# Another order of TensorE's work items in a segment-recurrent attention kernel on Trainium2

## The chip, the cores and the metric

One Trainium2 chip, of which the kernel uses one core. The metric is the time of one execution in device microseconds (us), and less is better. A core has five engines, each with an instruction queue of its own that is worked off in program order: TensorE (PE; its weight loads are listed as PEld), VectorE (DVE), ScalarE (ACT), GpSimd (POOL) and SyncE (SP), which issues most of the DMA transfers. They meet at semaphores: an instruction waits until those that produce its data, or free its buffer, have signalled. Matmul operands lie in the on-chip memory ("arena" in the trace), results in eight PSUM banks ("ps"), and 16 DMA engines carry data between the chip's HBM and the arena.

## What is computed

A memory-augmented attention layer and a gated feed-forward layer, mixed by a gate, over x of shape (1, 2048, 640) in bf16. The attention goes through 64 segments of 32 rows. Each puts 8 memory rows in front of its own (L = 40 rows), and its first 8 output rows are the memory of the next one, so segment s + 1 can't start its products before segment s has ended.

```python
for s in range(n_seg):                       # 64 segments, 32 heads of 192
    h = jnp.concatenate([mem, x[:, 32 * s:32 * s + 32, :]], axis=1)
    q, k, v = (jnp.einsum('btd,dhe->bhte', h, W) for W in (Wq, Wk, Wv))
    scores = jnp.einsum('bhqe,bhke->bhqk', q, k) * Dh ** -0.5
    scores = jnp.where(mask[None, None], scores, -1e9)
    o = jnp.einsum('bhqk,bhke->bhqe', softmax(scores), v)
    o = jnp.einsum('bhte,hed->btd', o, Wo)
    mem = o[:, :8, :]
    outs.append(o[:, 8:, :])
g = sigmoid((x * gate_w).sum(-1, keepdims=True))
out = g * concat(outs) + (1 - g) * ((gelu(x @ w_gate) * (x @ w_up)) @ w_down)
```

## The kernel before

The feed-forward layer is computed first, up to about 170 us. Then come the 64 segments, in groups of four. Segment s has the **type** s mod 4, and a planned order of TensorE items: the list `PROG` for types 0, 1 and 2, the list `PROG3` for type 3 (lines 524 to 545). `segment(s)` walks through the list, and each item emits its instructions on all engines that it concerns. Two items that are neighbours in the list follow each other on TensorE, and the copies and softmax steps that they emit stand in the same order on ScalarE, VectorE and GpSimd. A list is thus the schedule of every engine.

A tile has 32 columns and a segment 40 rows. The 8 memory rows and 24 of the segment's own go through the products of the segment itself; the other 8 own rows of each of a group's four segments, 32 in all, depend on x alone and make one block, the **left rows**, whose products are worked out ahead of the group.

The 32 heads are four **octets** of eight; octet numbers in the items count positions (0 to 3) in the segment, and the real octets come in reverse order in odd segments. The items:

- `g` n,k: slice k (0 to 4) of the contraction over 640, for product group n of `GROUPS`: group 0 is Q and K of octet 0; 1 is V 0, Q 1, K 1; 2 is V 1, Q 2, K 2; 3 is V 2, Q 3; 4 is K 3; 5 is V 3. A **product** is four matmuls of 128x384, one on each 32-column tile of the array (lines 1132, or 226 where the stationary operand is kept from the product before). Behind k = 4, ScalarE copies the results out of PSUM (line 1153 for Q and K, 1156 for V).
- `tq` i, `tk` i: VectorE transposes the Q or K rows of octet i into one buffer `Qs` or `Ks` (line 1170). As there is only one of each, the `tk` of the next octet waits for the scores of this one.
- `sc` i: mask (line 1181) and scores (1189, 234, 1196) of octet i on 64-column tiles, then maximum and subtraction on VectorE. `ex` i: the exponential on ScalarE (1220), then sum, reciprocal and two multiplications on VectorE (1222 to 1227).
- `pt` i: transposes of the probabilities (1243, 1248), copied out by ScalarE (1261; for the last octet half of it by VectorE). `pv` i: probabilities times V on 64-column tiles (1276, 1278), copied out by ScalarE (1308; for the last octet in halves, 1298 and 1302).
- `wo` i,h: half of octet i's part of the output product, in 32-column tiles for types 0 to 2 (lines 1326, and 1352 for the last octet), in 64-column tiles for type 3 (1370).
- `lf` t,u,k: done only in type t. A **left pair**, that is a Q and a K product (lines 924 and 226) for the left rows of a later group. `le` t,u,m: copy and transpose of such rows (1398). `vb` k, type 3 only: the V product of the next group's left rows for octet 0 (965).

In type 0 the product groups with V of octets 1 to 3 carry one product more per slice, that of the left rows, so that a slice of group 2 has four products and one of group 3 has three.

A segment ends with the last `wo`, the addition of partial sums and two transposes (1570) on VectorE, on which the next segment's first `g` waits. The `lf` and `le` items at the end of a list lie in that wait; `le` items behind the last `wo` are emitted after the segment's end steps.

Not all weights fit on chip. Of each pair of first-octet and fourth-octet pieces, 13 of Q, K, V (384 KB each) and three of Wo (480 KB) share a slot: as soon as an item has used up a piece that has a partner, `swap_loads` puts the partner's load into SyncE's queue (`load_piece`, line 629). So the fourth octet's K and V and the last Wo pieces of a segment are loaded within that segment, in the order in which the first octet's pieces come free, and its items wait for their landing.

```python
def swap_loads(seg, item):
    ...
    for key in done_keys:
        other = swap_in.get(key)
        if other is None or (other in partner) == (seg % 2 == 0):
            continue
        load_piece(other, "swap s%d" % seg)
```

Of the kernel before, what the change touches and what calls it, by code (L numbers as in the profile page):

```python
# [238 lines left out]
def _build(nc, A_x, A_mem0, A_Wq, A_Wk, A_Wv, A_Wo, seg_len, w_gate, w_up, w_down,  # L239
# [278 lines left out]
    def piece_view(key, o):  # L518
        if key[0] == 3:
# [1 line left out]
        return bview(o, GQ)  # L521

    GROUPS = [[(0, 0), (1, 0)], [(2, 0), (0, 1), (1, 1)], [(2, 1), (0, 2), (1, 2)], [(2, 2), (0, 3)], [(1, 3)], [(2, 3)]]
    PROG = [("g", 0, 0), ("g", 0, 1), ("g", 0, 2), ("g", 0, 3), ("g", 0, 4), ("tq", 0), ("g", 1, 0), ("g", 1, 1),
# [12 lines left out]
    PROG3 = [("g", 0, 0), ("g", 0, 1), ("g", 0, 2), ("g", 0, 3), ("g", 0, 4), ("g", 1, 0), ("tq", 0), ("tk", 0),  # L537
# [8 lines left out]
    PROGS = (PROG, PROG, PROG, PROG3)  # L546
    assert NOCT == 4
    WOP = 4
# [1065 lines left out]
def bass_gated_mix__memory_aug_recurrent_mem_tr__glu_gated_geglu__prompt_kernel(  # L1614
    nc,
    A_x,
    A_mem0,
    A_Wq,
    A_Wk,
    A_Wv,  # L1620
    A_Wo,
    A_seg_len,
    B_x,
    B_w_gate,
    B_w_up,
    B_w_down,
    gate_w,
    out,
):
    _build(nc, A_x, A_mem0, A_Wq, A_Wk, A_Wv, A_Wo, A_seg_len, B_w_gate, B_w_up, B_w_down, gate_w, out)  # L1630
# [33 lines left out]
```

## Time and profile before

| What | us |
|---|---|
| median of three runs | 1665.67 |
| lowest and highest of them | 1663.85, 1673.56 |
| the execution that was profiled | 1667.93 |
| its span, first to last instruction | 1666.2 |
| start of segment 0, start of segment 63 | 173.4, 1627.1 |
| mean segment of type 0, 1, 2, 3 | 23.6, 22.9, 22.1, 23.7 |

The rows below are of that profiled execution. In a row of the timeline stand the start in us from the span's start, the time from the first start to the last end of a run of equal instructions, engine, line, operation, tiles and shapes, the count (x), and in brackets an idle time of the engine just ahead with what ended it. Matmuls overlap each other, so the starts of two rows tell more than a duration. In a view by stretches there stand start and end, length, busy time of TensorE, weight loads, VectorE, ScalarE and GpSimd with instruction counts, the granted TensorE clock as a share of full speed, the share of time in which the 16 DMA engines are busy, and GB/s. A queue's row has packets, MB, and the share of the 16 engines' span. A DMA's row has its count, size and the us from issue to landing. The mean segments of the table come from the starts of each segment's first product.

### The profile page before, as it was taken

How to read it: one execution, taken by the hardware profiler on the slowest of the kernel's cores; microseconds unless marked ns; L12 is line 12 of the kernel's file. 1: busy time of each engine (PE TensorE's matmuls, PEld its weight loads, DVE VectorE, ACT ScalarE, POOL GpSimd, SP SyncE). 2: the span in 40 equal slices, each digit the busy share in tenths (PEclk: the TensorE clock that was granted, in tenths of full speed). 3: DMA queues.
4: the chain of work that ended last, by engine and by line, in shares of the span. 5: the costliest groups of instructions: out<-in, count | busy, mean ns of one | idle time of the engine just before them, and what ended most of it. 6: DMA issues, size and time to landing. Idle time of an engine off the chain costs nothing. (4 is left out here: it accounts for less than half of the span.)

```text
span 1666.2 us, 75811 instructions
## 1 busy us (share of the span) xinstructions
PE 1567.0 (94%) x37090; PEld 773.4 (46%) x28147; DVE 998.3 (60%) x3023; ACT 783.7 (47%) x1874; POOL 546.0 (33%) x1609
## 2 busy tenths in 40 slices
PE   9999899999999999999999999999999999999986
PEld 4444345444444445454444444454544444444543
DVE  6453566666566666666665666656665656656653
ACT  2222454545455454545454554545454555545452
POOL 1110233333333333333333333333333333333332
PEclk9999999999999999999999999999999999999998
DMA  9915999989899898989888898989888888988894
GB/s 292 345 47 157 321 319 324 317 315 313 310 323 334 299 323 292 331 317 332 299 310 302 317 343 283 313 290 326 322 296 309 301 326 318 316 292 311 312 326 163
DMA packets 275415, 499.28 MB, mean 300 GB/s; under 512 B 121119, under 2 KB 136327, under 8 KB 275079
## 3 DMA queue, kind: packets, MB, share of 16 engines
q1 hardware_dynamic: 271000, 491.30, 84.3%
q8 instruction: 255, 4.18, 1.0%
q10 hardware_dynamic: 4079, 3.14, 0.6%
q14 instruction: 81, 0.66, 0.1%
HBM read 473.25 MB, written 21.09 MB: 297 GB/s over the span
## 5 line engine op out<-in xcount | busy, mean ns | idle before, releaser
L1132 PE MATMUL ps<-arena 128*32 128x384 bf16 x8640 | 640.3, 329 | 19.6 <-DVE arena L1570 11.4
L226 PE MATMUL ps<-arena 128*32 128x384 bf16 x8960 | 635.9, 327 | 3.5 <-ACT arena L1153 1.2
L1132 PEld LDWEIGHTS ps<-arena 128*32 128x32 bf16 x8640 | 226.8, 96 | 390.8 <-issue 270.0
L1170 DVE STREAM_TRANSPOSE arena<-arena 128x384 bf16<-128x384 bf16 x512 | 273.7, 559 | 71.5 <-ACT arena L1153 70.2
L1153 ACT ACTIVATE arena<-ps 128x384 bf16<-128x384 f32 x512 | 230.3, 493 | 109.7 <-PE ps L1132 102.0
L1173 POOL COPY arena<-arena 64x160 bf16<-64x160 bf16 x256 | 81.3, 318 | 371.0 <-DVE arena L1170 368.9
L1326 PE MATMUL ps<-arena 128*32 128x320 bf16 x3456 | 180.9, 300 | 5.7 <-issue 3.2
L1156 ACT ACTIVATE arena<-ps 128x384 bf16<-128x384 f32 x256 | 124.9, 488 | 112.4 <-PE ps L1132 112.4
L1208 DVE TENSOR_REDUCE arena<-ps 104x4 f32<-104x160 f32 x256 | 83.0, 324 | 149.9 <-PE ps L1196 149.9
L1308 ACT ACTIVATE arena<-ps 128x480 bf16<-128x480 f32 (+1 forms) x208 | 116.6, 561 | 102.7 <-PE ps L1278 99.4
L1261 ACT ACTIVATE arena<-ps 128x448 bf16<-128x448 f32 x192 | 104.6, 545 | 122.8 <-PE ps L1248 122.6
L1006 POOL COPY arena<-arena 128x96 bf16<-128x96 bf16 x256 | 69.4, 271 | 231.1 <-PE ps L1196 159.4
L1222 DVE TENSOR_REDUCE arena<-ps 104x4 f32<-104x160 f32 x256 | 82.5, 322 | 97.6 <-ACT ps L1220 96.7
L1220 ACT ACTIVATE ps<-ps 104x160 f32<-104x160 f32 x256 | 75.7, 296 | 136.8 <-DVE ps L1210 134.9
L1370 PE MATMUL ps<-arena 128*64 128x320 bf16 x1536 | 124.9, 305 | 1.4 <-issue 0.6
L1276 PE MATMUL ps<-arena 128*64 128x160 bf16 x1536 | 119.0, 241 | 3.6 <-issue 3.5
L1326 PEld LDWEIGHTS ps<-arena 128*32 128x32 bf16 x3456 | 90.8, 96 | 47.2 <-ACT arena L1255 11.2
L924 PE MATMUL ps<-arena 128*32 128x384 bf16 x1280 | 108.7, 328 | 0.7 <-issue 0.7
L1278 PE MATMUL ps<-arena 128*64 128x64 bf16 x1536 | 104.3, 193 | 2.4 <-issue 2.1
L1316 POOL COPY arena<-arena 128x96 bf16<-128x96 bf16 x192 | 51.3, 267 | 162.7 <-ACT arena L1298 97.0
L1276 PEld LDWEIGHTS ps<-arena 128*64 128x64 bf16 x1536 | 81.7, 109 | 48.3 <-ACT arena L1156 19.4
L1398 ACT ACTIVATE arena<-ps 128x384 bf16<-128x384 f32 x120 | 57.2, 490 | 92.5 <-DVE arena L1570 41.4
(102 smaller groups left out, 2351.7 us busy)
## 6 DMA issues: line engine op xcount, KB each, us to landing
arena<-in_A_Wk_dram SPq DMA_DIRECT2D x335, 384.0 KB, 6.4
arena<-in_A_Wv_dram SPq DMA_DIRECT2D x335, 384.0 KB, 8.7
arena<-in_A_Wo_dram SPq DMA_DIRECT2D x205, 480.0 KB, 5.9
arena<-in_A_Wq_dram SPq DMA_DIRECT2D x209, 384.0 KB, 5.6
arena<-left_qk_scratch SPq DMA_DIRECT2D x126, 96.0 KB
left_qk_scratch<-arena SPq DMA_DIRECT2D x49, 192.0 KB, 5.2
left_qk_scratch<-arena SPq DMA_DIRECT2D x30, 96.0 KB, 5.5
ffn_b_scratch<-arena ACTq DMA_DIRECT2D x16, 160.0 KB, 4.1
```

Source lines behind the costliest of these rows:

```text
L226: return e.add_instruction(mybir.InstMatmult(name=nm, start_tensor_calc=like["start"], stop_tensor_calc=stop, tile_size=(128, 32), tile_po ...
L924: fns.append(lambda e, outp=outp, rhs=rhs, j=j: e.matmul(outp, lhs, rhs, start=(k == 0), stop=(k == KT - 1), tile_position=(0, 32 * j)))
L1132: fns.append(lambda e, outp=outp, rhs=rhs, j=j: e.matmul(outp, lhs, rhs, start=(k == 0), stop=(k == KT - 1), tile_position=(0, 32 * j)))
L1153: S_.add("act", lambda e, m=m, bk=bk: e.activation(out=rows_sb[m], in_=ps[:, bk, 0:384], func=ACTF.Copy), reads=[r_ps[bk]], writes=[r_rows ...
L1156: S_.add("act", lambda e, i=i, bk=bk: e.activation(out=v_sb[i % NVB].rearrange("p (c n) -> p c n", c=3), in_=ps[:, bk, 0:384].rearrange("p ...
L1170: S_.add("dve", lambda e: e.transpose(out=dst[:, :, 0:L], in_=rows_sb[m].rearrange("p (c r) -> p c r", r=L)), reads=[r_rows[m]], writes=[r ...
L1261: S_.add("act", lambda e: e.activation(out=PT, in_=ps[:, bank, 0:PTW + 128], func=ACTF.Copy), reads=[r_ps[bank]], writes=[r_PT], name="pT ...
L1276: return [lambda e: e.matmul(full, v[:, e0:e0 + 64], PTm[:, i], start=True, stop=False, tile_position=(0, 64 * i), skip_group_check=True), ...
L1278: lambda e: e.matmul(part, vl[:, e0:e0 + 64], PTl[:, i], start=False, stop=True, tile_position=(0, 64 * i), skip_group_check=True)]
L1308: S_.add("act", lambda e: e.activation(out=apx(u[:, 0, 0, :], [[rs, na], [3 * rs, 4], [1, R]]), in_=ps[:, A, 0:na * W].rearrange("p (c t r ...
L1326: fns.append(lambda e, i=i, t=t, j=j, gv=gv: e.matmul(ps[32 * j:32 * j + 32, bank, 0:2 * DJ].rearrange("p (h n) -> p h n", h=2), lhs2[i], ...
L1370: S_.add("pe", [lambda e, i=i, g_=g_, c=c, p=p: e.matmul(ps[64 * i:64 * i + 64, LB, 0:2 * DJ], U3[:, p % 4, c, :], g_[:, c, 2 * DJ * i:2 * ...
```

## The change

Only the two lists change; no item is added, dropped or altered. In `PROG` the K products of octet 3 (`g` 4,k) move ahead by one product group: `g` 4,0 follows `g` 3,4 directly, with `pt` 1, `sc` 2 and the left pair `lf` 1,0,4 behind it, where `sc` 2, `pv` 1 and `wo` 0,0 lay between. `pt` 0 comes one slice sooner and `sc` 1 two slices later; `pv` 0 stands straight behind `sc` 1 and ahead of `ex` 1; `tk` 3 and `g` 5,2 stand ahead of `pt` 2, and `wo` 1,1 next to `wo` 1,0. Left pairs are dealt anew: five of type 1's first unit lie among groups 2 to 4, those of the others behind K of octet 3, and `lf` 2,1,2 and `lf` 0,1,2 near the end, the latter between `pv` 3 and `wo` 3,0. Behind the last `wo` nothing changes within a type.

In `PROG3`, `tq` 0 and `tk` 0 come two and three slices later, `sc` 0 and `sc` 1 one later, `pt` 0 and `ex` 1 two sooner, `pv` 0 one sooner; `g` 4,0 to 4,2 stand ahead of `pt` 1 and `sc` 2; `wo` 0,0 stands behind `sc` 2, `wo` 2,0 next to `wo` 2,1; the third `vb` stands behind `wo` 3,1.

The order of SyncE's DMA issues is the same in both kernels; the queues of the other four engines are reordered along with the items.

```diff
--- before.py
+++ after.py
@@ -521,28 +521,28 @@
         return bview(o, GQ)
 
     GROUPS = [[(0, 0), (1, 0)], [(2, 0), (0, 1), (1, 1)], [(2, 1), (0, 2), (1, 2)], [(2, 2), (0, 3)], [(1, 3)], [(2, 3)]]
-    PROG = [("g", 0, 0), ("g", 0, 1), ("g", 0, 2), ("g", 0, 3), ("g", 0, 4), ("tq", 0), ("g", 1, 0), ("g", 1, 1),
-            ("tk", 0), ("g", 1, 2), ("sc", 0), ("g", 1, 3), ("ex", 0), ("g", 1, 4), ("g", 2, 0), ("g", 2, 1),
-            ("g", 2, 2), ("lf", 1, 0, 0), ("pt", 0), ("tq", 1), ("tk", 1), ("sc", 1), ("g", 2, 3), ("g", 2, 4),
-            ("tq", 2), ("ex", 1), ("lf", 2, 1, 0), ("lf", 1, 0, 1), ("lf", 1, 0, 2), ("pv", 0), ("g", 3, 0),
-            ("tk", 2), ("g", 3, 1), ("g", 3, 2), ("g", 3, 3), ("pt", 1), ("lf", 2, 1, 1), ("g", 3, 4), ("sc", 2),
-            ("ex", 2), ("lf", 2, 1, 2), ("pv", 1), ("wo", 0, 0), ("g", 4, 0), ("g", 4, 1), ("lf", 0, 1, 0),
-            ("g", 4, 2), ("lf", 1, 0, 3), ("lf", 1, 0, 4), ("lf", 1, 1, 0), ("lf", 1, 1, 1), ("le", 1, 0, 0),
-            ("tq", 3), ("g", 4, 3), ("le", 1, 0, 1), ("g", 4, 4), ("g", 5, 0), ("g", 5, 1), ("lf", 1, 1, 2),
-            ("lf", 0, 1, 1), ("pt", 2), ("wo", 0, 1), ("tk", 3), ("sc", 3), ("pv", 2), ("g", 5, 2), ("wo", 1, 0),
-            ("ex", 3), ("g", 5, 3), ("wo", 1, 1), ("g", 5, 4), ("wo", 2, 0), ("pt", 3), ("lf", 0, 1, 2),
-            ("wo", 2, 1), ("pv", 3), ("wo", 3, 0), ("wo", 3, 1), ("lf", 2, 1, 3), ("lf", 2, 1, 4), ("le", 2, 1, 0),
-            ("le", 2, 1, 1), ("lf", 1, 1, 3), ("lf", 1, 1, 4), ("le", 1, 1, 0), ("le", 1, 1, 1), ("lf", 0, 1, 3),
-            ("lf", 0, 1, 4), ("le", 0, 1, 0), ("le", 0, 1, 1)]
-    PROG3 = [("g", 0, 0), ("g", 0, 1), ("g", 0, 2), ("g", 0, 3), ("g", 0, 4), ("g", 1, 0), ("tq", 0), ("tk", 0),
-            ("g", 1, 1), ("g", 1, 2), ("sc", 0), ("g", 1, 3), ("ex", 0), ("g", 1, 4), ("tq", 1), ("g", 2, 0),
-            ("tk", 1), ("g", 2, 1), ("g", 2, 2), ("g", 2, 3), ("g", 2, 4), ("sc", 1), ("tk", 2), ("g", 3, 0),
-            ("pt", 0), ("tq", 2), ("g", 3, 1), ("g", 3, 2), ("g", 3, 3), ("ex", 1), ("pv", 0), ("g", 3, 4),
-            ("sc", 2), ("pt", 1), ("ex", 2), ("g", 4, 0), ("g", 4, 1), ("wo", 0, 0), ("g", 4, 2), ("g", 4, 3),
-            ("g", 4, 4), ("tq", 3), ("tk", 3), ("wo", 0, 1), ("pv", 1), ("sc", 3), ("g", 5, 0), ("pt", 2),
+    PROG = [("g", 0, 0), ("g", 0, 1), ("g", 0, 2), ("g", 0, 3), ("g", 0, 4), ("g", 1, 0), ("g", 1, 1), ("tq", 0),
+            ("g", 1, 2), ("tk", 0), ("sc", 0), ("g", 1, 3), ("ex", 0), ("g", 1, 4), ("g", 2, 0), ("tq", 1),
+            ("g", 2, 1), ("pt", 0), ("g", 2, 2), ("lf", 2, 1, 0), ("tk", 1), ("g", 2, 3), ("lf", 1, 0, 0),
+            ("lf", 1, 0, 1), ("g", 2, 4), ("sc", 1), ("tq", 2), ("pv", 0), ("lf", 1, 0, 2), ("g", 3, 0), ("g", 3, 1),
+            ("g", 3, 2), ("lf", 1, 0, 3), ("ex", 1), ("tk", 2), ("g", 3, 3), ("g", 3, 4), ("g", 4, 0),
+            ("lf", 1, 0, 4), ("pt", 1), ("sc", 2), ("g", 4, 1), ("tq", 3), ("ex", 2), ("g", 4, 2), ("pv", 1),
+            ("wo", 0, 0), ("lf", 2, 1, 1), ("g", 4, 3), ("le", 1, 0, 0), ("lf", 0, 1, 0), ("le", 1, 0, 1),
+            ("lf", 1, 1, 0), ("g", 4, 4), ("lf", 1, 1, 1), ("g", 5, 0), ("g", 5, 1), ("tk", 3), ("lf", 0, 1, 1),
+            ("lf", 1, 1, 2), ("g", 5, 2), ("pt", 2), ("wo", 0, 1), ("sc", 3), ("pv", 2), ("wo", 1, 0), ("wo", 1, 1),
+            ("g", 5, 3), ("ex", 3), ("lf", 2, 1, 2), ("g", 5, 4), ("wo", 2, 0), ("pt", 3), ("wo", 2, 1), ("pv", 3),
+            ("lf", 0, 1, 2), ("wo", 3, 0), ("wo", 3, 1), ("lf", 1, 1, 3), ("lf", 2, 1, 3), ("lf", 2, 1, 4),
+            ("le", 2, 1, 0), ("lf", 0, 1, 3), ("lf", 0, 1, 4), ("lf", 1, 1, 4), ("le", 2, 1, 1), ("le", 0, 1, 0),
+            ("le", 0, 1, 1), ("le", 1, 1, 0), ("le", 1, 1, 1)]
+    PROG3 = [("g", 0, 0), ("g", 0, 1), ("g", 0, 2), ("g", 0, 3), ("g", 0, 4), ("g", 1, 0), ("g", 1, 1), ("g", 1, 2),
+            ("tq", 0), ("g", 1, 3), ("tk", 0), ("sc", 0), ("ex", 0), ("g", 1, 4), ("g", 2, 0), ("g", 2, 1),
+            ("g", 2, 2), ("tq", 1), ("tk", 1), ("g", 2, 3), ("pt", 0), ("g", 2, 4), ("g", 3, 0), ("sc", 1),
+            ("g", 3, 1), ("tq", 2), ("ex", 1), ("g", 3, 2), ("pv", 0), ("g", 3, 3), ("tk", 2), ("g", 3, 4),
+            ("g", 4, 0), ("g", 4, 1), ("g", 4, 2), ("pt", 1), ("g", 4, 3), ("sc", 2), ("wo", 0, 0), ("tq", 3),
+            ("ex", 2), ("g", 4, 4), ("wo", 0, 1), ("pv", 1), ("g", 5, 0), ("tk", 3), ("pt", 2), ("sc", 3),
             ("wo", 1, 0), ("wo", 1, 1), ("ex", 3), ("pv", 2), ("g", 5, 1), ("g", 5, 2), ("g", 5, 3), ("pt", 3),
-            ("wo", 2, 0), ("g", 5, 4), ("wo", 2, 1), ("pv", 3), ("vb", 0), ("vb", 1), ("vb", 2), ("wo", 3, 0),
-            ("wo", 3, 1), ("vb", 3), ("vb", 4)]
+            ("g", 5, 4), ("wo", 2, 0), ("wo", 2, 1), ("pv", 3), ("vb", 0), ("vb", 1), ("wo", 3, 0), ("wo", 3, 1),
+            ("vb", 2), ("vb", 3), ("vb", 4)]
     PROGS = (PROG, PROG, PROG, PROG3)
     assert NOCT == 4
     WOP = 4
```

## Prediction, made before the changed kernel ran

> **What bounds the kernel now.** I read the page's busy times and queues first, then stretches of one group of four segments (28 to 31, types 0 to 3), then TensorE's timeline inside them. From the page:
>
> ```profile
> span 1666.2 us, 75811 instructions
> ...
> PE 1567.0 (94%) x37090; PEld 773.4 (46%) x28147; DVE 998.3 (60%) x3023; ACT 783.7 (47%) x1874; POOL 546.0 (33%) x1609
> ...
> q1 hardware_dynamic: 271000, 491.30, 84.3%
> ```
>
> Two things are near full, TensorE and the weight transfers, so the question is which ends last in a segment. The view by stretches, once for whole segments and once for the middle of each (start and end, length, busy time of the five engines, granted clock, DMA share, GB/s):
>
> ```profile
> 818.13:841.50 23.37, 22.39 (x612) 11.45 (x473) 15.65 (x49) 10.72 (x28) 7.89 (x24) 1.00 0.86 300
> 841.50:864.60 23.10, 21.95 (x594) 10.09 (x434) 14.67 (x47) 12.41 (x31) 7.95 (x24) 1.00 0.90 317
> 864.60:886.98 22.38, 20.55 (x553) 9.72 (x413) 13.77 (x45) 11.47 (x29) 7.88 (x24) 1.00 0.93 326
> 886.98:911.31 24.33, 22.85 (x510) 11.87 (x388) 13.18 (x43) 11.82 (x29) 9.40 (x26) 1.00 0.85 295
> ```
>
> ```profile
> 820.60:839.40 18.80, 18.09 (x492) 9.60 (x388) 11.93 (x38) 9.39 (x24) 5.78 (x17) 1.00 0.98 352
> 844.50:863.20 18.70, 17.76 (x496) 8.87 (x380) 11.70 (x38) 10.54 (x26) 5.96 (x19) 1.00 1.01 359
> 867.60:885.90 18.30, 16.51 (x456) 8.51 (x360) 10.84 (x36) 9.61 (x24) 6.19 (x20) 1.00 1.00 363
> 889.98:909.00 19.02, 18.16 (x417) 10.11 (x335) 9.91 (x33) 9.10 (x22) 7.32 (x20) 1.00 0.97 347
> ```
>
> Per segment there are 18.3 to 19.0 us in which the DMA engines have no free time (share 0.97 to 1.01), framed by a few us in which they have. That stretch starts when the first group has used up its weights, and it ends at the last Wo piece. The change moves nothing in the first group before `sc` 0 of types 0 to 2, and the order of DMA issues on SyncE is the same before and after. So the stretch stays; TensorE can gain only what it does not already lose waiting for a landing. TensorE's timeline in segment 30 (type 2) shows such waits, and the price of the pieces that move:
>
> ```profile
> 875.56 0.33 PE L1132 MATMUL ps<-arena 128*32 128x384 bf16 x4
> 875.72 0.34 PE L226 MATMUL ps<-arena 128*32 128x384 bf16 x4
> 875.99 0.25 PE L1181 MATMUL ps<-arena 128*40 128x160 bf16 x2
> 876.07 0.26 PE L1189 MATMUL ps<-arena 128*40 128x40 bf16 x8
> ...
> 876.25 0.18 PE L1196 MATMUL ps<-arena 128*40 128x40 bf16 x1
> 876.36 0.35 PE L924 MATMUL ps<-arena 128*32 128x384 bf16 x4
> ...
> 879.38 0.33 PE L1181 MATMUL ps<-arena 128*40 128x160 bf16 x2
> 879.83 0.28 PE L1189 MATMUL ps<-arena 128*40 128x40 bf16 x8
> ...
> 880.03 0.18 PE L1196 MATMUL ps<-arena 128*40 128x40 bf16 x1
> 880.05 0.24 PE L1276 MATMUL ps<-arena 128*64 128x160 bf16 x2
> ...
> 884.58 0.81 PE L1352 MATMUL ps<-arena 128*32 128x160 bf16 x36 [0.43 <-DVE arena L1302]
> 885.94 0.39 PE L1352 MATMUL ps<-arena 128*32 128x160 bf16 x12 [0.56 <-DMA arena<-in_A_Wo_dram]
> ```
>
> Starts count here, not durations. A product (four matmuls on 32-column tiles) takes 875.72 - 875.56 = 0.16. Going to the scores' wider tiles takes 0.27 instead (875.72 to 875.99), and going back 0.11 (876.25 to 876.36), where scores to PV, both wide, takes 0.02 (880.03 to 880.05). So a wide block between narrow ones costs 0.11 + 0.09 = 0.20 of switching. Mask to scores takes 0.08 at 875.99, but 0.45 at 879.38: `sc` 3 waits 0.37 for the last K rows, turned late. `wo` 3 waits 0.43 for the last head's output, and its last quarter 0.56 for a Wo transfer: in this segment the transfers end last.
>
> **The change part by part.** Type 2 first. *K of octet 3 sooner*: `g` 4,0 to 4,2 now stand ahead of `pv` 1, so `tk` 3 is done before `sc` 3: -0.37. *Softmax of octet 0*: `pt` 0 now follows `g` 2,1 instead of `g` 2,2 and a left product.
>
> ```profile
> 870.14 0.18 DVE L1227 TENSOR_TENSOR arena<-ps,arena 104x32 bf16<-104x32 f32 x1
> ...
> 870.18 0.34 PE L1132 MATMUL ps<-arena 128*32 128x384 bf16 x4
> ```
>
> `g` 2,1 is through at 870.18, the probabilities at 870.14 + 0.18 = 870.32: with 0.05 to pass it on, a new wait of 0.19. *Softmax of octet 1*: `pv` 0 now stands straight behind `sc` 1, and `ex` 1 behind it, so the copy of `pv` 0's result is ahead of the exponential on ScalarE. The rows of that chain now:
>
> ```profile
> 872.57 0.49 ACT L1156 ACTIVATE arena<-ps 128x384 bf16<-128x384 f32 x1 [1.04 <-PE ps L1132]
> 872.67 0.34 PE L924 MATMUL ps<-arena 128*32 128x384 bf16 x4
> 872.96 0.87 ACT L1153 ACTIVATE arena<-ps 128x384 bf16<-128x384 f32 x2
> 873.70 0.32 ACT L1220 ACTIVATE ps<-ps 104x160 f32<-104x160 f32 x1
> 873.92 0.58 ACT L1308 ACTIVATE arena<-ps 128x480 bf16<-128x480 f32 x1
> ...
> 874.89 0.18 DVE L1227 TENSOR_TENSOR arena<-ps,arena 104x32 bf16<-104x32 f32 x1
> 874.99 0.57 DVE L1170 STREAM_TRANSPOSE arena<-arena 128x384 bf16<-128x384 bf16 x1
> ```
>
> Count from 872.67, the end of `g` 2,4. The three copies end at 872.96 + 0.87, 1.16 later; then the 0.58 copy, of which about 0.55 until the next starts; then from the exponential's start to the probabilities 874.89 + 0.18 - 873.70 = 1.37. So `pt` 1 is ready at 3.1. TensorE gets there after switching 0.11, mask and scores 0.28, PV with its switch back 0.41 (880.05 and the like), and eleven products of 0.16: 2.6. New wait 0.5, with `sc` 2, `pv` 1, `wo` 0,0 and the rest of K queued behind it. `sc` 2 stands directly behind `pt` 1; it needs the K rows that VectorE turns next, done 0.49 after the probabilities (874.99 + 0.57 - 875.07), while TensorE arrives 0.28 after `pt` 1's start: 0.2 more. *V*: `g` 5,2 stands right behind `g` 5,1, 1.3 us of `pt` 2 to `pv` 2 earlier. Its piece lands late:
>
> ```profile
> 869.58 2.80 SPq L629 DMA_DIRECT2D arena<-in_A_Wv_dram  x5
> ...
> 877.64 1.31 PE L1132 MATMUL ps<-arena 128*32 128x384 bf16 x28
> ```
>
> ```profile
> arena<-in_A_Wv_dram SPq DMA_DIRECT2D x1, 384.0 KB, 8.4
> ```
>
> The third of the five V issues (the DMA view for 870.85 to 871.10) takes 8.4 us: landing at 879.3. The 28 matmuls are `g` 4,0 to 5,1; seven products after 877.64 is 878.8. In the new order one left pair (0.33) is out of the way and the waits above (0.9) are in it: 879.3 again, so this wait is the other face of the same 0.9, not an addition. Sum for type 2 on TensorE: 0.19 + 0.5 + 0.2 - 0.37 = +0.5, bounded by -0.37 and +0.9. It is covered by the 0.56 for which the Wo piece is late anyway: 0. If that cover is gone, it costs the 0.5.
>
> Type 1 has the same `pt` 0 (+0.19). Between `pv` 0 and `pt` 1 it has six left products more (1.0), so no wait there. For `sc` 3 its segment shows no wait at all, where type 2 has 0.37:
>
> ```profile
> 857.48 0.25 PE L1181 MATMUL ps<-arena 128*40 128x160 bf16 x2
> 857.57 0.27 PE L1189 MATMUL ps<-arena 128*40 128x40 bf16 x8
> ```
>
> Between 0 and -0.37 I take -0.2. Behind `sc` 3 one product fewer (0.16) now covers the softmax before `pt` 3, and V's third piece is wanted 1.3 us sooner: between 0 and +0.5 for both, I take +0.1, nearest to the one product. Sum +0.1. Type 0 has three or four products per step, which cover `pt` 0 and `pt` 1. New there is `pv` 1: `pt` 1 comes one product after `g` 3,4, and its copy stands behind the copies of V and Q (0.39 + 0.49, the rows at 872.57 and 872.96) and takes about as long as the 0.49 or 0.58 ones: ready 1.4 to 1.5 after `g` 3,4, wanted at about 1.2. Between 0 and +0.3, I take +0.25, by the copies' rows. The left pair `lf` 0,1,2 between `pv` 3 and `wo` 3 fills 0.33 of a wait like the 0.43 above, but no longer covers the copy ahead of `pv` 3: between -0.33 and 0, I take -0.2. Sum +0.05.
>
> Type 3 is where the wide tiles matter, since its `wo` is wide too. By the two lists it has ten wide blocks now (`sc` 0, `sc` 1, `pv` 0, `sc` 2, `wo` 0,0, then `wo` 0,1 with `pv` 1 and `sc` 3, and so on) and eight after: `wo` 0,0 joins `sc` 2, and `wo` 2,0 joins 2,1. 2 x 0.20 = -0.40. Against it, the fourth octet's K and last V are wanted sooner, and K is late already:
>
> ```profile
> 900.08 0.35 PE L1132 MATMUL ps<-arena 128*32 128x384 bf16 x4 [0.86 <-DMA arena<-in_A_Wk_dram]
> ```
>
> A piece that lands when it did ends the wait at the same moment; what comes sooner only waits longer. Between 0 and +0.4 (nothing of the saving left), I take +0.2, the middle, since this segment loses 0.86 and the group's other three show no K wait among the rows above. The third `vb` behind `wo` 3,1 instead of ahead makes one wait 0.16 longer and the next 0.16 shorter. Sum -0.2.
>
> All: (0.05 + 0.1 + 0 - 0.2) x 16 groups = -0.8 us. The profiled run took 1667.93 (span 1666.2 and 1.7 around it), 2.3 over the median of three, 1665.67. Made against the profiled run the sum gives 1667.1, brought to the median **1665**.
>
> The row for the cover says 363 GB/s at a share of 1.00. [...]
>
> **The rivals.** *Slower: the cover gives out.* If the Wo piece is not late in most segments of types 1 and 2, `pt` 0, `pt` 1 and `sc` 2 count: 0.5 in type 2, 0.35 in type 1 (with V's piece), 0.05 in type 0, 0 in type 3, 0.9 x 16 = +14: **1680**. It decides from the point where the wait at 885.94 is under 0.5; here it is 0.56, with 0.06 to spare, and the chain of softmax is read from rows. *Faster: TensorE is the bound after all.* For it: 94% busy, and only one Wo wait in the rows. Then the late `sc` 3 (0.37 in types 1 and 2), the filled 0.33 in type 0 and the 0.40 in type 3 count and the new waits shrink to `pt` 0: (1.47 - 0.38) x 16 = -17: **1648**. Against it: the shares of 0.97 to 1.01. *Nothing moves:* every segment ends with its transfers, 1666; for the measurement the same case as my forecast.
>
> **How the numbers follow.** 1% is 17 us, about what a measurement of this kernel can tell from no change. Forecast and "nothing moves" 0.70, slower rival 0.18, faster 0.12. The range goes from the faster rival, 1648, to the slower one with type 0's 0.3 on top (+5), 1685; outside is less than 2 in 10. The rivals' middle values lie at the 1% line, and with their spread: faster by over 1% 0.12, within 0.70, slower 0.18.
>
> **What would show it.** In type 2: TensorE's row of `pt` 1 (L1243) with an idle of about 0.5, mask to scores back at 0.08 for octet 3, the last Wo row still behind a DMA. In type 3: L1370 right behind L1196. Transfers: the same GB/s and share. I am wrong if the middle stretch itself shortens or lengthens, or if type 2 grows by 0.5 with no Wo wait left.

## The result and the profile after

| | us |
|---|---|
| before, median of 20 runs (lowest to highest) | 1671.47 (1663.85 to 1677.42) |
| changed, median of 20 runs (lowest to highest) | 1676.45 (1668.09 to 1687.07) |
| ratio, 95% interval | 1.0035 (1.0019 to 1.0050) |
| profiled executions, before and changed | 1667.93, 1677.87 |
| mean segment of type 0, 1, 2, 3, before | 23.60, 22.93, 22.10, 23.70 |
| mean segment of type 0, 1, 2, 3, changed | 23.74, 23.36, 22.39, 23.48 |

By the ratio the changed kernel is slower by 0.35%, some 6 us (the two medians lie 5.0 apart). The two profiled executions lie 9.9 apart, more than the medians, so the means of the segments show where, and the experiments how much. Types 0, 1 and 2 lost, type 3 gained.

The page of the changed kernel:

```profile
span 1676.1 us, 76054 instructions
...
PE 1567.9 (94%) x37107; PEld 763.3 (46%) x28147; DVE 987.0 (59%) x3023; ACT 782.8 (47%) x1874; POOL 548.5 (33%) x1609
...
q1 hardware_dynamic: 271000, 491.30, 83.9%
q8 instruction: 255, 4.18, 1.0%
```

TensorE is as busy as before to 0.9 us; the other 9.0 of the 9.9 us between the profiles are idle time. The view of TensorE's waits adds them up (who waited for what: us in total, times, longest). Before:

```profile
PE ps L1352 <- ACT arena L1298: 6.8, 14, 0.5
PE ps L1352 <- DMA arena<-in_A_Wo_dram: 5.6, 12, 0.8
PE ps L1352 <- issue: 4.7, 6, 1.3
PE ps L1276 <- issue: 3.5, 5, 1.3
PE ps L1326 <- issue: 3.2, 8, 0.7
PE ps L1132 <- issue: 3.2, 5, 1.1
PE ps L1181 <- POOL arena L1173: 2.9, 13, 0.3
PE ps L1132 <- DMA arena<-in_A_Wv_dram: 2.3, 5, 0.7
...
PE ps L1132 <- DMA arena<-in_A_Wk_dram: 1.4, 2, 0.9
```

Changed:

```profile
PE ps L1132 <- DMA arena<-in_A_Wv_dram: 16.2, 29, 1.0
...
PE ps L1132 <- DMA arena<-in_A_Wk_dram: 7.2, 15, 1.1
PE ps L1278 <- issue: 5.5, 7, 1.3
PE ps L1326 <- issue: 5.4, 7, 1.3
...
PE ps L1352 <- DMA arena<-in_A_Wo_dram: 2.4, 5, 0.9
...
PE ps L1352 <- ACT arena L1298: 1.0, 2, 0.5
```

Waits for weights rose from 10 to 27 us in all rows together, waits for other engines fell by 8 (ScalarE's copies of `pv` 3 from 6.8 to 1.0; the row of the masks, line 1181, behind GpSimd's copies of line 1173, 2.9, is gone), and the rows with "issue" (nothing that the profile shows was waited for) sum to 22.0 in both. By these totals the obvious reading is that the V and K products now come ahead of their weights. The middle of segment 30, in stretches (columns as before):

```profile
883.43:901.43 18.00, 16.65 (x464) 8.16 (x372) 10.67 (x36) 9.70 (x24) 6.09 (x19) 1.00 1.00 369
```

The stretch of full DMA engines is what it was, 18 us at a share of 1.00. Inside it, TensorE's timeline:

```profile
891.23 0.25 PE L1181 MATMUL ps<-arena 128*40 128x160 bf16 x2
891.51 0.27 PE L1189 MATMUL ps<-arena 128*40 128x40 bf16 x8
...
893.62 1.11 PE L1132 MATMUL ps<-arena 128*32 128x384 bf16 x16
895.34 0.35 PE L1132 MATMUL ps<-arena 128*32 128x384 bf16 x4 [0.61 <-DMA arena<-in_A_Wv_dram]
...
896.12 0.25 PE L1181 MATMUL ps<-arena 128*40 128x160 bf16 x2
896.21 0.26 PE L1189 MATMUL ps<-arena 128*40 128x40 bf16 x8
...
900.67 1.01 PE L1352 MATMUL ps<-arena 128*32 128x160 bf16 x48 [0.43 <-DVE arena L1302]
```

`sc` 2 now waits (mask to scores 0.28), `sc` 3 no longer does (0.09, forecast 0.08), the third V piece is waited for, and all 48 matmuls of `wo` 3 run in one piece: the 0.56 behind the last Wo piece is gone. In type 1 another kind of wait stands out, in segment 29:

```profile
873.09 0.24 PE L1276 MATMUL ps<-arena 128*64 128x160 bf16 x2
874.62 0.22 PE L1278 MATMUL ps<-arena 128*64 128x64 bf16 x2 [1.29 <-issue]
```

In the middle of `pv` 2 TensorE stands still for 1.29, with nothing that the profile shows to wait for. Type 3 shows what was forecast of it, `wo` 0,0 right behind `sc` 2, 0.02 after its last row:

```profile
913.19 0.18 PE L1196 MATMUL ps<-arena 128*40 128x40 bf16 x1
913.21 0.98 PE L1370 MATMUL ps<-arena 128*64 128x320 bf16 x12
```

### The profile page after: what moved, and what is told of

It is laid out like the page before. It is cut to its first block, busy times and chain, and to the rows that moved or that the text cites. A ratio compares the mean times of both kernels' runs of the same rounds, so it can differ in the third digit from the quotient of the medians.

```text
span 1676.1 us, 76054 instructions
## 1 busy us (share of the span) xinstructions
PE 1567.9 (94%) x37107; PEld 763.3 (46%) x28147; DVE 987.0 (59%) x3023; ACT 782.8 (47%) x1874; POOL 548.5 (33%) x1609
## 3 DMA queue, kind: packets, MB, share of 16 engines
q8 instruction: 255, 4.18, 1.0%
## 4 chain that ended last, share of the span: by engine, by line
PE 65%; DMA 19%; DVE 5%; SPq 4%; issue 3%; ACT 3%; POOL 0%; DVEq 0%; POOLq 0%; ACTq 0%
PE ps L1132 17%; PE ps L226 15%; DMA arena<-in_A_Wv_dram 11%; PE ps L1370 6%; PE ps L1326 6%; DMA arena<-in_A_Wk_dram 6%; PE ps L1276 3%; PE ps L924 3%; PE ps L1352 3%; PE ps L1181 2%; DMA arena<-in_A_Wo_dram 2%; SPq L629 2%; PE ps L830 2%; PE ps L833 2%; PE ps L856 1%
## 5 line engine op out<-in xcount | busy, mean ns | idle before, releaser
L1132 PE MATMUL ps<-arena 128*32 128x384 bf16 x8640 | 652.2, 329 | 36.4 <-DMA arena<-in_A_Wv_dram 16.2
L226 PE MATMUL ps<-arena 128*32 128x384 bf16 x8960 | 643.5, 327 | 3.2 <-ACT arena L1153 1.0
L1132 PEld LDWEIGHTS ps<-arena 128*32 128x32 bf16 x8640 | 226.7, 96 | 437.4 <-issue 294.8
L1170 DVE STREAM_TRANSPOSE arena<-arena 128x384 bf16<-128x384 bf16 x512 | 277.4, 561 | 54.3 <-ACT arena L1153 52.9
L1326 PE MATMUL ps<-arena 128*32 128x320 bf16 x3456 | 176.4, 300 | 8.8 <-issue 5.4
L1370 PE MATMUL ps<-arena 128*64 128x320 bf16 x1536 | 121.2, 304 | 0.5 <-ACT arena L1308 0.5
L924 PE MATMUL ps<-arena 128*32 128x384 bf16 x1280 | 112.6, 331 | 1.7 <-issue 1.7
L1326 PEld LDWEIGHTS ps<-arena 128*32 128x32 bf16 x3456 | 84.2, 96 | 49.2 <-ACT arena L1255 15.9
```

The source lines that it names most:

```text
L226: return e.add_instruction(mybir.InstMatmult(name=nm, start_tensor_calc=like["start"], stop_tensor_calc=stop, tile_size=(128, 32), tile_po ...
L924: fns.append(lambda e, outp=outp, rhs=rhs, j=j: e.matmul(outp, lhs, rhs, start=(k == 0), stop=(k == KT - 1), tile_position=(0, 32 * j)))
L1132: fns.append(lambda e, outp=outp, rhs=rhs, j=j: e.matmul(outp, lhs, rhs, start=(k == 0), stop=(k == KT - 1), tile_position=(0, 32 * j)))
L1170: S_.add("dve", lambda e: e.transpose(out=dst[:, :, 0:L], in_=rows_sb[m].rearrange("p (c r) -> p c r", r=L)), reads=[r_rows[m]], writes=[r ...
L1326: fns.append(lambda e, i=i, t=t, j=j, gv=gv: e.matmul(ps[32 * j:32 * j + 32, bank, 0:2 * DJ].rearrange("p (h n) -> p h n", h=2), lhs2[i], ...
L1370: S_.add("pe", [lambda e, i=i, g_=g_, c=c, p=p: e.matmul(ps[64 * i:64 * i + 64, LB, 0:2 * DJ], U3[:, p % 4, c, :], g_[:, c, 2 * DJ * i:2 * ...
```

## The experiments

Two explanations stood at the start. Theory A: the loss is TensorE waiting for V and K weights. Rival B: the new softmax waits are the loss. All ratios are to the kernel before, run on the same chip in the same rounds.

### One list at a time

e1_list3_only takes the new `PROG3` with the old `PROG`, e2_list012_only the new `PROG` with the old `PROG3`.

> Only the type 3 list is the new one, types 0 to 2 keep the old list. In the two profiles type 3 went from a mean of 23.70 to 23.48, types 0, 1 and 2 from 23.60, 22.93, 22.10 to 23.74, 23.36, 22.39. Theory A (the loss is TensorE waiting for transfers in types 1 and 2, type 3 gains by fewer changes of tile width): -0.2 x 15 = -3 us, ratio to before about 0.998, type 3 at 23.5, the others as before. Rival B (new softmax waits are the loss, the lists of all types alike): type 3 gains nothing, ratio 1.000 or above.

> Only the list of types 0 to 2 is the new one, type 3 keeps the old list. Theory A: the measured +5 and the -3 of type 3 add up, so +8 us, ratio 1.005; waits of TensorE for V transfers about 16 us as in the changed kernel (2.3 before), for K transfers about 1.4 as before. Rival B: +5 us, ratio 1.003, since type 3 is no part of it.

Measured: 0.9965 (0.9935 to 0.9995) and 1.0056 (1.0031 to 1.0082), both near what theory A expected. Within their intervals the parts add up to the whole, so the list of types 0 to 2 costs about 9 us and the list of type 3 saves 4 to 6. In e1's profile type 3 is at 23.27.

### The V product alone

e3_v2_back against the changed kernel:

```diff
-("lf", 1, 1, 2), ("g", 5, 2), ("pt", 2), ("wo", 0, 1), ("sc", 3), ("pv", 2), ("wo", 1, 0),
+("lf", 1, 1, 2), ("pt", 2), ("wo", 0, 1), ("sc", 3), ("pv", 2), ("g", 5, 2), ("wo", 1, 0),
```

e4_v2_forward against the kernel before:

```diff
-("lf", 0, 1, 1), ("pt", 2), ("wo", 0, 1), ("tk", 3), ("sc", 3), ("pv", 2), ("g", 5, 2),
+("lf", 0, 1, 1), ("g", 5, 2), ("pt", 2), ("wo", 0, 1), ("tk", 3), ("sc", 3), ("pv", 2),
```

> The changed kernel with one item back: g 5,2 behind pv 2 instead of ahead of pt 2, in the list of types 0 to 2. Theory A: the second V wait of type 2 (0.78 in the mean) goes and the waits for V transfers fall from 16 to about 6 us; some of it comes back at the last Wo piece, which has 0.2 to 0.3 us of slack in type 2; time 4 to 8 us under the changed kernel, ratio to before 0.999 to 1.001. Rival B (softmax waits ahead of pt 0, pt 1 and sc 2 are the cost, the V wait only takes them in): nothing changes, ratio 1.0035.

> The kernel before with that one item moved: g 5,2 ahead of pt 2, nothing else. Theory A: in type 2 its piece lands at 14.76 after the segment's start and TensorE would be there at about 14.2, so a wait of 0.5 in type 2 (16 segments: V waits from 2.3 to about 10 us); the 0.37 ahead of sc 3 and the 0.4 at the last Wo piece cover a part, so the time grows by 0 to 5 us, ratio 1.000 to 1.003. Rival B: no change within 1 us and no growth of the V waits beyond 3 us.

Measured: e3 1.0050 (1.0022 to 1.0078), no faster than the changed kernel; e4 1.0006 (0.9977 to 1.0035). In e3 the waits behaved as theory A says and the time didn't. e4 decides nothing: its time lies in the 1.000 to 1.003 that theory A allowed. From the waits of e3:

```profile
PE ps L1326 <- issue: 13.3, 15, 2.4
...
PE ps L1352 <- DMA arena<-in_A_Wo_dram: 7.1, 13, 1.2
PE ps L1132 <- DMA arena<-in_A_Wv_dram: 6.3, 12, 0.8
```

V waits fell from 16.2 to 6.3, Wo waits rose from 2.4 to 7.1, and the rows with "issue" sum to 31.9 instead of 22.0. (The profiled execution took 1687.95, 9 us over the median of e3, so its totals may be high.) In e4 V waits rose (2.3 to 9.2), as expected, while the time stayed within its interval. By e3 theory A falls as the whole cause of the loss: a wait for V that goes comes back as another wait.

### No reloads of K and V

```diff
 def load_piece(key, name):
     loaded[slot_id[key]] = key
+    if name.startswith("swap") and key[0] in (1, 2):
+        return
```

> The kernel before, with the reloads of K and V pieces left out in all segments (10 of 13 swaps; their products use whatever lies in the slot), so that no K or V product can wait for a transfer and the Wo pieces land some 9 us sooner. Theory A: the 10 us for which TensorE waited for transfers in the profile go, or a part of it moves to the waits behind; 1655 to 1662 us.

> The changed kernel with the same reloads left out. Theory A: the 26.5 us for which TensorE waited for transfers go, 16.5 more than in the kernel before, so this one is faster than the kernel before without reloads by 8 to 12 us: the new order is the better one where transfers are no limit. Rival B (the new softmax waits cost the time): it stays slower than the kernel before without reloads by about 5 us or more.

Measured: 0.9772 (0.9749 to 0.9794) for the old order and 0.9762 (0.9738 to 0.9785) for the new one. Both theories miss: the two orders are equal within the interval, where A wanted 8 to 12 us and B the opposite. So without these transfers neither order is the better one, to within 0.3%. And the saving of e5 was 38 us, where only 10 us of waits for weights had been there. Rows with "issue" fell from 22.0 to 4.1, so the transfers bring about most of them. (TensorE's busy time also fell by 11 us, from 1567.0 to 1556.1; the cause of that stays open.) Type 1 is 0.5 longer with the new order here as well (22.86 against 22.33), with other types shorter. Waits for Wo, e5 and then e6 (two added lines make L1352 L1354 here, and in the kernels with added instructions below):

```profile
PE ps L1354 <- DMA arena<-in_A_Wo_dram: 5.0, 9, 1.1
```

```profile
PE ps L1354 <- DMA arena<-in_A_Wo_dram: 9.8, 20, 1.2
```

With the new list `wo` 0,0 of type 1 comes 1.1 us later, and with it the load of the second Wo piece (issued at 14.1 instead of 13.0 after the segment's start, medians); the last one lands at 21.7 instead of 20.2, and TensorE stands idle for it, by over 0.06 us, in 14 of 16 segments.

### What "issue" is

The trace has a row for every DMA packet, also for those of the queue "q8 instruction" above: 255 of 16,384 bytes, 4.18 MB, each some 1.0 us long. I numbered TensorE's instructions as the trace lists them (matmuls, weight loads and the 57 or 72 rows of semaphores and drains) and took the rows with "issue" above 0.2 us.

```
kernel                stalls   place modulo 256   end of stall behind the end of a q8 packet
before                35       176 or 177, all    1.2 to 1.6 us, all
changed               30       193 or 194, all    1.2 to 1.6 us, all
e3_v2_back            42       176 or 177, all    1.2 to 1.6 us, all
```

(The numbers 177 and 194 differ since the trace of before lacks 17 matmul records.) 255 packets of 256 are 65,280 instructions, and the trace of before lists 65,309 for TensorE. By these counts TensorE's instructions arrive in packets of 256, and an "issue" above 0.2 us is TensorE at the boundary of two packets with the next one not there. In the segments it runs 256 instructions in a median of 5.9 us; the packet for the next 256 starts a median of 2.2 (before) and 2.5 us (changed) after the last boundary, and takes 1.0 and then 1.4 until TensorE goes on. Taken boundary by boundary, the median left to spare is 0.8 and 0.6; in e5, without the K and V transfers, it is 2.4. Most crossings show no such stall, but 35 of the 255 of before show one above 0.2 us, and the 22.0 us of all rows with "issue" are not small against the change, some 6 us.

Theory F: these boundaries lie at fixed instructions of a segment, and it matters which items stand there. A group of four segments has 3970 of the listed instructions, 15 packets and 130 more, so that the boundaries alternate between two sets of places, half a packet apart. In type 1 of the changed kernel the late ones lie at 17.5 us in one set, mostly in `pv` 2, and at 20 us in the other, mostly in `wo` 2,1 (means). Instructions added at the very start move them:

```diff
                    reads=[r_ident], writes=[r_ps[4]], name="ffn warm")
+            S_.add("pe", [lambda e: e.matmul(ps[:, 4, 0:64], ident, ident[:, 0:64], start=True, stop=True) for _ in range(32)],
+                   reads=[r_ident], writes=[r_ps[4]], name="pad")
```

(64 in the place of 32 for 128 instructions.) e10 instead gives type 1 its old list back.

> The kernel before with 32 small matmuls (64 instructions with their weight loads) added to the warm-up at the very start, nothing else. Theory F (TensorE's instructions come in packets of 256 by DMA, and its stalls without a releaser are late packets): the 256-instruction boundaries fall on other items of every segment, a quarter of a packet away, so the stalls change from 22 us by 4 us or more in either direction and the time follows by as much; the stalled instructions keep one and the same number modulo 256. Rival (the stalls come with the items themselves, or by chance): 22 us within 3, time within 2 us of before, the added matmuls included.

> The changed kernel with the same 64 instructions at the start. Theory F: stalls away from 22 us by 4 us or more, time away from the changed kernel's ratio of 1.0035 by as much. Rival: ratio 1.0035 to 1.005.

> The changed kernel with 128 instructions at the start. A group of four segments has 3970 of TensorE's instructions in the trace, 15 packets and 130 more, so that the boundaries of one group lie half a packet from those of the next; 128 more instructions only exchange the two. Control for theory F: stalls 22 us within 4, ratio as without them, 1.0035 (plus up to 0.002 for the added matmuls). The rival expects the same here.

> The changed kernel with the old list for type 1 alone (types 0 and 2 the new list, type 3 the new one). In the profiles the new list costs type 1 0.5 a segment, 0.3 of it in stalls without a releaser. If that loss belongs to the list: -8 us against the changed kernel, ratio to before 0.9985 to 1.000. If it is a matter of where the packet boundaries happen to lie, not of the list: 1.003 to 1.005.

| run | ratio (95%) | "issue", us | of it in type 1 | mean segment of type 1 |
|---|---|---|---|---|
| changed | 1.0035 (1.0019 to 1.0050) | 22.0 | 11.0 | 23.36 |
| e9, 128 more | 1.0031 (1.0012 to 1.0049) | 25.1 | 14.9 | 23.58 |
| e8, 64 more | 0.9997 (0.9981 to 1.0014) | 14.2 | 1.9 | 22.67 |
| e10, old list for type 1 | 0.9979 (0.9958 to 1.0000) | 14.0 | 4.5 | 22.70 |
| before | 1 | 22.0 | 5.5 | 22.93 |
| e7, before and 64 more | 1.0001 (0.9980 to 1.0023) | 24.8 | 7.5 | 23.03 |

64 instructions that compute nothing take the whole loss away, and 128, which put the boundaries back on the same places, leave it. e10 comes out as if the loss belonged to the list of type 1, but it can't tell, since the old list also puts other items at the boundaries. From the waits of e9, the control:

```profile
PE ps L1328 <- issue: 10.3, 10, 1.9
```

From the waits of e8:

```profile
PE ps L1134 <- DMA arena<-in_A_Wv_dram: 15.2, 29, 0.8
...
PE ps L1354 <- DMA arena<-in_A_Wo_dram: 6.4, 10, 1.2
...
PE ps L1354 <- issue: 4.7, 5, 1.8
PE ps L1328 <- issue: 3.3, 5, 1.5
```

The V waits are all still there, 15.2 us, at no loss of time against the kernel before. For the kernel before, e7, theory F expected a total at least 4 us away and found nearly the same one (24.8, ratio 1.0001): the places change there too, but the old lists do about as badly at either. At the moved places the two orders are thus level (e7 1.0001, e8 0.9997): the new one has 10.6 us less of "issue" there and 18.5 us more of waits for weights. So the loss belongs neither to the order nor to the places alone, but to this order at these places.

One thing goes with it that no run here separates. In the profiles the granted clock falls to 0.50 for 3.4 or 6.8 us at a time: within segments 0 to 62 once in before (at 199 us, for 6.8) and three times in the changed kernel (at 223, 595 and 971 us, for 3.4 each), each time 1.1 to 1.8 us behind a stall with "issue" of 0.7 to 1.3 us. Most stalls above 0.2 us are followed by none (34 of 35 in before, 27 of 30 in the changed kernel), so the link is not shown. The mean granted clock is 0.9935 over the 20 runs of the changed kernel, 0.9941 in e9 and 0.9949 in e8, and 0.9949 to 0.9953 for the kernel before in the experiments; by the largest difference, 0.9953 less 0.9935, 0.0018 x 1670 = 3.0 of the 6 us can be the clock (an estimate).

### Both together

> The kernel e3_v2_back (the changed lists with g 5,2 behind pv 2) with the 64 instructions at the start. In e3_v2_back the waits for V transfers fell to 6.3 us and stalls on instruction packets rose to 31.9, 17.2 of them in type 1. With the boundaries moved, theory F expects type 1's stalls at 2 to 5 us as in e8_after_pad64 (1.9), and the transfer theory then has its gain: V waits 6 us instead of 15, time 4 to 8 us under e8_after_pad64 (ratio 0.9997), so 0.995 to 0.998. Rival (the last Wo piece of type 2 takes over what V gives up): waits for Wo grow by as much and the ratio stays at 0.999 to 1.001.

> Old list for types 0 and 2, new list for types 1 and 3, and the 64 instructions at the start: in each type the list whose segments were shorter where the packet boundaries lay well (type 0 23.5 old, type 1 22.67 new in e8_after_pad64 against 22.8 to 23.0 old, type 2 22.1 to 22.5 old, type 3 23.4 new against 23.7). By these: 0.994 to 0.998, waits for V transfers under 3 us. If boundaries and lists don't add up like this: 0.998 to 1.001.

Measured: e11 1.0001 (0.9970 to 1.0032), e12 0.9986 (0.9958 to 1.0014). From the waits of e11:

```profile
PE ps L1354 <- DMA arena<-in_A_Wo_dram: 9.4, 20, 1.0
...
PE ps L1328 <- issue: 8.9, 12, 1.8
PE ps L1354 <- issue: 8.6, 11, 1.4
...
PE ps L1134 <- DMA arena<-in_A_Wv_dram: 3.4, 8, 0.7
```

V waits fell by 12 us and gave nothing: Wo waits took 3 of them and instruction packets 12 (26.0 instead of 14.2), while type 1 stayed short (22.61). In type 2 waits for Wo rose from 2.3 us in e8 to 5.7. The best lists by type don't add up either (e12): its "issue" rows sum to 21.2. Of all versions that load every weight e1_list3_only is the fastest, 0.35% under the kernel before, at an interval that just leaves out 1; that, and e10 at its edge, beat both kernels.

## Why the prediction was wrong

The time, 1676.45, is within 1% of before and in the range, but the forecast was a gain of 0.8 us and it is a loss of some 6. That the range holds it says little, since the range is 37 us wide. And of the 11.4 us between the forecast 1665 and the result, 5.8 lie in the base: it was the median of three runs, 1665.67, and the median of 20 is 1671.47.

**Where it failed: the sum for type 1, +0.1.** It priced waits for results and for weights and had no term for TensorE's own instruction stream. Measured are +0.43 a segment in the two profiles (and 23.36 in e2 against 22.79 in e1). The rows with "issue" in type 1 went from 5.5 to 11.0 us over 16 segments, +0.34 each; e8 and e10 take that away and with it 6 and 9 us. The "issue" rows stood in the waits of before, 22.0 us, and the prediction says nothing of them. What it did price came out near its figures (means over type 1): the wait ahead of `pt` 0 is about 0.25 longer (forecast 0.19), the one in `sc` 3 0.23 shorter (0.2), the one ahead of `pt` 3 0.17 longer (0.1), and one in `sc` 1 that it did not price 0.14 shorter. Together that is about +0.05, beside the forecast +0.1.

The stalls grew at both late boundaries, in two ways. "Ready" is here the end of the packet and the 1.4 us behind it. Up to the boundary at 17.5, 256 instructions took 5.22 us before and take 4.80 now, without the stall (`sc` 3 no longer waits, products stand elsewhere), and the packet is ready only after 5.7 and 5.5 (means over seven segments): here the new order spends waiting for instructions what it saves on TensorE. That is the smaller part, stalls of 5.1 us after 3.3. Up to the boundary at 20 the 256 instructions take what they took (4.89 before, 4.99 now; eight segments), but the packet is ready after 5.60 instead of 4.95, since it starts 3.25 instead of 2.54 after the last boundary: stalls of 5.4 us after 1.6. Why it starts later there stays open.

**Type 2, forecast 0** (a new +0.5, covered). The prices had been read from one group of four segments. Over all segments of type 2 `sc` 3 waited 0.25 in the mean, not 0.37, and gave that; the Wo wait of 0.56, the cover, stood in 8 of 16 segments, 3.3 us in all or 0.2 a segment (0.3 us now). The 0.2 forecast for `sc` 2 came (the 0.28 above, less 0.08), and `pt` 0 cost 0.25, a little over its 0.19. But the prediction missed that `sc` 1, too, waited in the old order (mask to scores 0.49 in the mean, 0.08 now), and that `pt` 1 already had a wait of about 0.27, the same as now: TensorE comes to V sooner than worked out. "This wait is the other face of the same 0.9, not an addition" was therefore wrong in size, since waits for V in type 2 take 1.0 a segment (15.3 us, 0.9 before). It was right in kind: e3 and e11 take most of that wait out, and the time stays. The remaining 0.3 of type 2 in the profiles is not settled: its waits for V grew by 14.4 us and its other waits fell by 8.4, but in e8, at the time of before, type 2 is at 22.65, and in e11, with 3.1 us of waits for V, at 22.41.

**Type 3, forecast -0.2**: of the kernels with all reloads eight with the new list have 23.27 to 23.49, four with the old one 23.43 to 23.87, means 23.42 and 23.66, so -0.24; e1 measures the gain alone. The cost was where it was put, in K: 7.2 us of waits for K, all in type 3, 1.4 before. (The 0.86 that the prediction read was one of only two such waits.) **Type 0, forecast +0.05**: 23.74 in both kernels with all the new lists for types 0 to 2 (changed, e2) against 23.60 and 23.65 (before, e1), +0.12; over all profiles with all reloads the new list has 23.63 to 24.11 and the old one 23.49 to 23.79.

**The bound.** "The stretch stays" held: share 1.00 over 18.0 us, and e5 shows how much hangs on it, 38 us. But "the order of DMA issues is the same" does not mean the same times: in type 1 the Wo loads wait for `wo` 0,0, which moved 1.1 us back. With the boundaries out of the way (e8) this is the next thing that TensorE meets in type 1, so far a small one: waits for Wo of 2.6 us there, 0.9 in the changed kernel.

**The rivals.** The slower one, with its cover giving out in types 1 and 2, named the right direction and the wrong mechanism. It needed type 2 without a Wo wait, which came (3.3 us before, 0.3 now), and the softmax waits as the loss, which did not: in e6 those waits are there and the two orders are level. The faster one fell since TensorE's gains go into waits for weights and instructions.

## What to carry to other kernels

In this kernel, where transfers fill the DMA engines for 18.0 us of a segment (share 1.00, segment 30), TensorE has a third limit beside its work and its operands: its own instruction stream, 255 packets that the page counts among those of the 16 DMA engines (queue q8, 1.0% of their span). Its rows with "issue" are 22.0 us, and 4.1 without the reloads of K and V (e5). All stalls above 0.2 us, 35 in before and 30 in the changed kernel, fall on one place modulo 256 (176 or 177, 193 or 194). So where a trace shows idle time of TensorE without a releaser, number its instructions and see whether it falls on one such place before a reordering is priced, and compare two orders at two or more positions of the boundaries (a few dummy instructions at the start; 64 took 0.38% off the changed kernel) before one is called better. A wait for a transfer that a reordering removed was worth nothing here, since other waits took its place: e11 has 12 us of V waits less than e8, 3 more for Wo and 12 more of "issue", at 1.0001 after 0.9997. And read a price from all segments of a type, not from one.

## What the runs showed of the hardware

- With the DMA engines full (share 1.00 in the middle of segment 30), the next packet of instructions was ready 5.0 to 5.9 us after the last boundary at the late boundaries of type 1 (means in before, changed and e9; single ones 4.4 to 6.7), where 256 instructions took TensorE 4.8 to 5.3 us without the stall. Without K and V reloads (e5) the packet starts 1.0 us after the boundary (median) instead of 2.2.
- In the segments 242 of 246 packets (before) and 245 (changed) start only after the boundary ahead of the one at which they are needed, and each stall above 0.2 us ended 1.2 to 1.6 us behind the end of such a packet.
- 64 added instructions at the start of the changed kernel took 0.38% off its time, with the same work in the same order (1.0035 to 0.9997; 1.0031 to 0.9997 in the same rounds).
